# First-stage attention scores in float32 from 64-row halves, and transposes as pairs of 64-row halves

## The chip, the cores and the metric

One core of a Trainium2 chip runs the whole program. The metric is device microseconds (us) of one execution; smaller is better. The engines are called as the profile calls them: PE is TensorE (matmuls), PEld its weight loads, DVE VectorE, ACT ScalarE, POOL GpSimd, SP SyncE (here it only issues DMAs).

## The reference

Two attention stages follow each other. The first has 8 batches of 8 heads, 576 positions, head width 64, and keeps only scores within `tau` of the row's maximum. Its output, 512 wide per position, goes into a mixture of four causal attention experts, of which each position takes the best two.

```
scores = scale * q @ k.T                      # stage 1, per batch and head
thresh = max(scores) - tau
scores = where(scores >= thresh, scores, -1e9)
attn = exp(scores - max); attn /= sum(attn) + 1e-9
x = (attn @ v), heads side by side            # (8, 576, 512)

logits = x @ w_gate; top 2 of 4 experts, weights w by softmax
for e in range(4):                            # stage 2, per batch
    q, k, v = x @ wq[e], x @ wk[e], x @ wv[e]
    a = softmax(scale * q @ k.T, causal)
    out += (e in top 2) * w * (a @ v @ wo[e])
```

## The kernel before

**Tiles.** Stage 1 works on 32 pairs of heads, four per batch. The 576 positions are four tiles of 128 queries (s = 0 to 3) and a tail of 64, and the tails of the two heads make one tile of 128 rows (s = 4). For each pair `prep` (L827) loads q and k, `scores` (L903) makes scores, maximum, threshold, exponential and normalised weights, `transp` (L945) and `transp_tails` (L958) transpose the weights on PE and copy them out of PSUM with ACT, and `attnv` (L972) multiplies them with v. After the four pairs of a batch, `moe` (L1222) runs stage 2 for that batch: projections, values and gate, then for two pairs of experts (ep) and five query tiles `scores2` (L1110), `transp2` (L1151) and `attnv2`, and `output`.

**Scores before.** From the third pair on (`DIRECT = 2`) q and k are transposed on PE, split into a rounded high part and a rest (`hl`, ACT and DVE in `split`), and spread by DMA (`spread_keys`, `spread_queries`) into `qt` and `kt`, so that one matmul with 128 rows multiplies both parts of q with one part of k. A tile s < 4 takes, for each head, four such matmuls of 288 columns in the one-pass format fp32r; s = 4 takes six. Each head of a tile has its own two PSUM banks (family `s`) and its own place in the order. The first two pairs (`first`, L777) go another way: plain float32, head 0 in rows 0 to 63 and head 1 in rows 64 to 127 of the array, four matmuls of 64 rows for a tile; the chip gets a float32 matmul as two instructions, so that the trace shows eight.

**Stage 2 scores before.** `spread2` (L1052) spreads the parts of q and k by DMA in the same manner; a head of a tile takes two fp32r matmuls with 128 rows.

**Transposes before.** A 128x128 block is one `transpose` (L594): the block is the stationary operand, the identity moves through it, 128 columns. Four blocks fill one PSUM bank (family `g`), which one ACT copy empties.

**Order.** The functions only record operations. `Plan.arrange` then gives each engine's instructions an order and each tile a buffer, from a modelled cost of each operation and from places (`PLACE`, `PLACE_OP`), numbers that say how early each unit of work ranks. All matmuls into one PSUM tile form a group that PE runs in one piece; PE may take groups up to three places out of order (`AHEAD`). A group starts when its PSUM banks are free: there are eight of 2 KB per partition. In the profile all matmuls have line L591 and all transposes L1282; DMAs have L688 and L690.

Of the kernel before, what the change touches and what calls it, by code (L numbers as in the profile page):

```python
# [22 lines left out]
SLOTS = {"ki": 1, "qi": 1, "tm": 2, "hl": 1, "qt": 2, "kt": 2, "pp": 4, "st": 2, "vm": 2, "p2": 3, "pt": 10,  # L23
         "ptt": 2, "x": 12, "v2": 1, "q2": 2, "q2x": 1, "k2x": 1, "zt": 2, "z0": 2, "z1": 2, "pt2t": 1}
PLACE = {
# [45 lines left out]
}  # L71
PLACE_OP = {
    "ACT gw": -1.321, "ACT hl": -2.1489, "ACT lg": 0.5171, "ACT p2": -0.0353, "ACT pp": 0.2646, "ACT pt": 0.2207,
    "ACT ptt": -0.0387, "ACT q2": 1.5521, "ACT q2d0": 4.5817, "ACT q2d1": 1.7694, "ACT tau_t": -0.2988,
    "ACT tm": -1.4854, "ACT v2": 1.2109, "ACT warm": -1.1366, "ACT wkh": 0.8714, "ACT woh": 1.1122,
    "ACT wqh": 1.1708, "ACT wvh": 1.067, "ACT x": -0.5607, "ACT z0": 1.1015, "ACT z1": -0.3179, "ACT zt": 0.2316,
    "DVE col": 0.6337, "DVE g": -1.4561, "DVE gate": -1.9949, "DVE gt": -3.3295, "DVE gw": 0.1335,
    "DVE hl": -3.6827, "DVE lg": 2.0741, "DVE p2": 0.0604, "DVE pp": -1.0396, "DVE pt": -0.5423,
    "DVE pt2t": 1.7323, "DVE q2": 0.9391, "DVE qsc": -0.1751, "DVE s": -0.5422, "DVE st": -1.8452,
    "DVE still": -0.1359, "DVE tau_n": -1.4713, "DVE v2": -0.8112, "DVE warm": -2.9831, "DVE x": 0.2785,  # L80
    "DVE z0": -0.7041, "DVE z1": -2.1009, "DVE zt": 0.323, "POOL col": 0.0444, "POOL hl": 1.0723,
    "POOL ident": -1.4208, "POOL mask": -3.3156, "POOL mask2": -1.1591, "POOL p2": 0.2278, "POOL pp": 1.6676,
    "POOL pt2t": 0.6725, "POOL q2d0": 1.5757, "POOL q2d1": 1.1287, "POOL qd0": 1.6629, "POOL qd1": 1.472,
    "POOL qi": 2.1477, "POOL st": 0.0218, "POOL tie": -1.6109, "POOL tm": -0.3646, "POOL vtz0": 0.7892,
    "POOL vtz1": -0.4386, "POOL wkl": 1.9586, "POOL wol": 0.1773, "POOL wql": 3.2786, "POOL wvh": 1.4077,
# [62 lines left out]
class Op:  # L148
    def __init__(self, e, busy, late, outs, ins, fn, at):
# [1163 lines left out]
```

## Time and profile before

| | us |
|---|---|
| runs of the kernel, median of 3 (lowest, highest) | 914.93 (914.17, 915.96) |
| span of the profiled execution, first to last instruction | 911.6 |
| PE, PEld busy | 892.5, 832.6 |
| DVE, ACT, POOL busy | 734.2, 651.4, 442.7 |

The profile gives its execution by the span. The median of the runs is 3.3 us above it, which is what lies around the span. Busy time of PE counts a matmul from its start to its modelled end, and matmuls overlap; what one costs in a stream is the distance from its start to the start of the next.

### The profile page before, as it was taken

How to read it: one execution, taken by the hardware profiler on the slowest of the kernel's cores; microseconds unless marked ns; L12 is line 12 of the kernel's file. 1: busy time of each engine (PE TensorE's matmuls, PEld its weight loads, DVE VectorE, ACT ScalarE, POOL GpSimd, SP SyncE). 2: the span in 40 equal slices, each digit the busy share in tenths (PEclk: the TensorE clock that was granted, in tenths of full speed). 3: DMA queues.
4: the chain of work that ended last, by engine and by line, in shares of the span. 5: the costliest groups of instructions: out<-in, count | busy, mean ns of one | idle time of the engine just before them, and what ended most of it. 6: DMA issues, size and time to landing. Idle time of an engine off the chain costs nothing.

```text
span 911.6 us, 26016 instructions
## 1 busy us (share of the span) xinstructions
PE 892.5 (98%) x9218; PEld 832.6 (91%) x9218; DVE 734.2 (81%) x2139; ACT 651.4 (71%) x1542; POOL 442.7 (49%) x905
## 2 busy tenths in 40 slices
PE   7899999999999999999999999999999999999998
PEld 5589999899999999999999999999999999999986
DVE  6887778896888869888698877988778886888375
ACT  4787668775778757887587865888667875777454
POOL 5867436553455535555255543555435653445101
PEclk9999999999999999999999999999999999999999
DMA  7625474554565554754546555564474554561151
GB/s 175 163 68 139 116 173 102 142 140 110 143 157 136 135 127 104 189 147 116 127 104 175 127 127 144 127 168 121 103 181 116 141 143 117 138 153 42 36 140 59
DMA packets 147650, 117.86 MB, mean 129 GB/s; under 512 B 99008, under 2 KB 107456, under 8 KB 147520
## 3 DMA queue, kind: packets, MB, share of 16 engines
q1 hardware_dynamic: 146176, 115.90, 51.6%
q8 instruction: 73, 1.20, 0.6%
q10 hardware_dynamic: 1344, 0.30, 0.2%
q14 instruction: 57, 0.47, 0.2%
HBM read 30.42 MB, written 9.44 MB: 44 GB/s over the span
## 4 chain that ended last, share of the span: by engine, by line
PE 81%; DVE 6%; ACT 4%; SPq 3%; DMA 2%; issue 2%; POOL 1%; DVEq 0%; ACTq 0%
PE banks L591 60%; PE banks L1282 20%; SPq L688 2%; ACT pp L678 2%; DMA k2x<-q 1%; DVE pp L662 1%; ACT p L678 1%; DVE col L648 1%; ACT pt L612 1%; DVE gt L614 1%; SPq L690 0%; DVE banks L667 0%; DVE gw L623 0%; DVE q L623 0%; DVE x L623 0%
## 5 line engine op out<-in xcount | busy, mean ns | idle before, releaser
L640 POOL TENSOR_SCALAR pp<-pp,col 128x576 f32<-128x576 f32 x278 | 205.5, 749 | 171.3 <-DVE col L651 132.6
L648 DVE TENSOR_REDUCE col<-banks 128x1 f32<-128x576 f32 x304 | 227.1, 751 | 34.5 <-PE banks L591 31.9
L662 DVE SCALAR_TENSOR_TENSOR pp<-banks,col,pp 128x576 f32<-128x576 f32 x278 | 223.6, 813 | 29.9 <-ACT pp L678 17.1
L612 ACT ACTIVATE pt<-banks 128x512 f32<-128x512 f32 (+2 forms) x400 | 223.1, 590 | 32.9 <-PE banks L1282 29.4
L678 ACT ACTIVATE pp<-banks,col 128x576 f32<-128x576 f32 x284 | 207.2, 740 | 40.0 <-DVE col L648 36.1
L1282 PE MATMUL banks<-ident,pp 128*128 128x128 f32 x1281 | 186.4, 274 | 3.0 <-DVE p L662 1.8
L591 PE MATMUL banks<-kt,qt 128*128 128x288 f32 x960 | 174.9, 311 | 0.4 <-DMA tm<-in_k_dram 0.3
L640 POOL TENSOR_SCALAR col<-col,tau_n 128x1 f32<-128x1 f32 x288 | 77.0, 268 | 193.9 <-DVE col L648 150.3
L1282 PEld LDWEIGHTS banks<-ident,pp 128*128 128x128 f32 x1281 | 148.7, 140 | 13.6 <-issue 3.8
L591 PE MATMUL banks<-pt,vm 128*64 128x128 f32 (+1 forms) x2560 | 154.6, 264 | 0.0
L591 PEld LDWEIGHTS banks<-kt,qt 128*128 128x128 f32 x960 | 136.0, 189 | 6.1 <-issue 3.1
L591 PEld LDWEIGHTS banks<-pt,vm 128*64 128x64 f32 x2560 | 131.3, 137 | 7.7 <-issue 4.3
L678 ACT ACTIVATE p<-banks,col 128x256 f32<-128x256 f32 (+4 forms) x142 | 78.7, 561 | 33.1 <-DVE col L667 18.5
L640 POOL TENSOR_SCALAR p<-p,col,gw 128x384 f32<-128x384 f32 (+3 forms) x117 | 71.6, 621 | 57.1 <-ACT p L678 32.5
L612 ACT ACTIVATE x<-banks 128x256 fp32r<-128x256 f32 (+1 forms) x96 | 28.3, 329 | 70.5 <-PE banks L591 70.5
L1282 PE MATMUL banks<-ident,p 128*128 128x128 f32 x404 | 63.2, 276 | 3.3 <-POOL p L640 1.8
L591 PE MATMUL banks<-wvh,x 128*128 128x260 f32 x320 | 64.2, 284 | 0.0
L667 DVE CUSTOM_DVE_ANT_0 banks<-banks,mask 128x384 f32<-128x384 f32 (+3 forms) x128 | 61.9, 500 | 2.4 <-PE banks L591 1.3
L591 PE MATMUL banks<-ptt,vtz 128*64 128x128 f32 (+1 forms) x640 | 58.9, 262 | 0.0
L623 DVE TENSOR_TENSOR x<-banks,x 128x256 fp32r<-128x256 f32 (+1 forms) x96 | 31.9, 353 | 31.2 <-ACT x L612 30.8
L639 DVE TENSOR_SCALAR col<-col 128x2 f32<-128x2 f32 (+1 forms) x240 | 47.8, 202 | 10.4 <-ACT p L678 8.0
L1282 PEld LDWEIGHTS banks<-ident,p 128*128 128x128 f32 x404 | 47.1, 141 | 9.3 <-POOL p L640 3.0
(139 smaller groups left out, 1558.2 us busy)
## 6 DMA issues: line engine op xcount, KB each, us to landing
kt<-hl SPq DMA_DIRECT2D x240, 144.0 KB, 2.6
k2x<-q SPq DMA_DIRECT2D x128, 128.0 KB, 2.4
qt<-hl SPq DMA_DIRECT2D x120, 128.0 KB, 2.4
vm<-in_v_dram SPq DMA_DIRECT2D x32, 256.0 KB, 3.1
q2x<-q SPq DMA_DIRECT2D x64, 128.0 KB, 2.4
qi<-in_q_dram SPq DMA_DIRECT2D x60, 128.0 KB, 2.5
ki<-in_k_dram SPq DMA_DIRECT2D x60, 128.0 KB, 3.0
out_dram<-st SPq DMA_DIRECT2D x30, 256.0 KB, 2.5
```

The lines of the kernel that those rows point to most:

```text
L591: lambda o, x, y: nc.tensor.matmul(o, x, y, start=start, stop=stop))
L612: run(e, t, [dst], [src], lambda d, s: nc.scalar.activation(d, s, AF.Copy))
L614: run(e, t, [dst], [src], lambda d, s: nc.vector.tensor_copy(d, s))
L623: lambda d, a, b: (nc.vector if e == "DVE" else nc.gpsimd).tensor_tensor(d, a, b, op=op))
L639: return m.tensor_scalar(d, s, x_, None, op0=op0)
L640: return m.tensor_scalar(d, s, x_, y_, op0=op0, op1=op1)
L648: lambda d, s: nc.vector.tensor_reduce(d, s, axis=axis, op=op, **({"negate": True} if negate else {})))
L662: return nc.vector.scalar_tensor_tensor(d, a_, x_, r.pop(0), op0=op0, op1=op1, **kw)
L667: lambda o, a, i, m: nc.vector.tensor_tensor_reduce(o, i, m, 1.0, 3e38, ALU.add, ALU.min, a))
L678: return nc.scalar.activation(d, s, AF.Exp, scale=scale, **kw)
L688: fn = lambda d, s: q_.dma_start(d.bitcast(F32), s.bitcast(F32))
L1282: o.fn(*(r.place() for r in (*o.outs, *o.ins)))
```

## The change

The special path for the first two pairs goes, and every pair takes one path: q and k (and their tails, loaded into the diagonal blocks of the 128x128 tiles `tk` and `tq`, which hold zeros elsewhere) are transposed, copied by ACT into `kx` and `qx` (ACT multiplies q by the scale on the way), and multiplied in float32 from 64-row halves, both heads of a tile side by side, in one group of four PSUM banks. The tail tile uses 64-column halves of the array instead. A transpose of a 128x128 block becomes two of 64 rows each, into two banks, which two ACT copies empty into interleaved columns. The second stage multiplies its fp32r parts in place, three products for each head from 64-row halves, with no spreading. The transposes of s = 4 go together with the tails of the first group, and those of the second stage are grouped by `T2_GROUPS`. The places are other numbers throughout; `SLOTS` has other buffers (five `pp` instead of four).

```diff
+    def transposed(x, y, blocks):
+        for n, (a, b) in enumerate(blocks):
+            for o, i, sl in ((x, a, heads[0]), (y, b, heads[1])):
+                half_transpose(o[:, n * D:(n + 1) * D], i[sl], sl)
+    def half_transpose(o, x, rows):
+        plan.op("PE", 30, 30 + 217 + 35, [o], [x, ident[rows, rows]], nc.tensor.transpose)
...
     def prep(n):
-        hl = plan.tile("hl", [P, 2, 2 * SM + 3 * ST], F32R)
...
+        for j in range(2):
+            dma(tk[heads[j], heads[j]], k[b, 2 * hp + j, SM:, :], "SP", more)
...
+            if x is ki:
+                transposed(*gs, list(zip([*cs, tail], [tail, *cs])))
+            else:
+                transposed(*gs, [(c, c) for c in (*cs, tail)])
...
+                copy("ACT", d, g, None if x is ki else qsc)
     def scores(n, s, qk):
+        sp = [plan.tile("s", [P, 2, 512], F32) for _ in range(nj)]
+        sp[-1].v.first = sp[0].v
+        for hf in range(2):
+            for j, rows in enumerate(heads):
+                o = hf * HS + (ST if j == 0 else 0)
+                if s < R:
+                    matmul(sp[j][:, hf, :HS], qx[rows, s * P:(s + 1) * P], kx[rows, o:o + HS], True, True)
+                else:
+                    matmul(sp[0][rows, hf, :HS], qx[:, SM + j * ST:SM + (j + 1) * ST], kx[:, o:o + HS], True, True)
...
+    def blocks_out(blocks, out):
+        gs = [gbank() for _ in range(2)]
+        gs[1].v.first = gs[0].v
+        transposed(*gs, blocks)
+        w = len(blocks) * D
+        for i, g in enumerate(gs):
+            copy("ACT", out[:, :2 * w].rearrange("p (n c) -> p n c", c=P)[:, :, i * D:(i + 1) * D],
+                 g[:, :w].rearrange("p (n c) -> p n c", c=D))
     def transp(n, s, pp):
+        cols = [j * (S + ST) + c * P for j in range(2) for c in range(R)]
+        return blocks_out([(pp[:, o:o + P],) * 2 for o in cols], plan.tile("pt", [P, 2 * SM], F32))
...
-    def spread2(qs, ks):
...
     def scores2(b, t, ep, q2, gates, place):
+            for i, (x, y) in enumerate(HHL):
+                for g, rows in zip(gs, heads):
+                    matmul(g, q2[0][rows, x, t * P:w], q2[1][rows, y, :w], i == 0, i == 2)
...
+T2_GROUPS = ((4,), (3,), (2,), (1, 0))
```

## Rows read from the trace of the kernel before

**Rows 1.** The page: span, and busy time of each engine.

```profile
span 911.6 us, 26016 instructions
PE 892.5 (98%) x9218; PEld 832.6 (91%) x9218; DVE 734.2 (81%) x2139; ACT 651.4 (71%) x1542; POOL 442.7 (49%) x905
```

**Rows 2.** Windows: stretch, length, busy PE, PEld, DVE, ACT, POOL, clock, DMA, GB/s.

```profile
279.80:389.00 109.20, 109.06 (x1150) 103.78 (x1150) 90.76 (x265) 80.13 (x191) 53.88 (x110) 1.00 0.55 136
825.80:911.60 85.80, 79.70 (x766) 72.05 (x762) 50.94 (x171) 47.92 (x132) 18.20 (x31) 1.00 0.24 66
...
20.00:40.00 20.00, 15.67 (x90) 10.04 (x86) 17.41 (x48) 14.19 (x29) 15.14 (x32) 1.00 0.68 169
```

**Rows 3.** Groups by form: transposes on PE, the two largest and the smallest.

```profile
L1282 PE MATMUL banks<-ident,pp 128*128 128x128 f32 x1281 | 186.4, 274 | 3.0 <-DVE p L662 1.8 <-ACT ptt L612 0.6 <-POOL pp L640 0.3
...
L1282 PE MATMUL banks<-ident,p 128*128 128x128 f32 x404 | 63.2, 276 | 3.3 <-POOL p L640 1.8 <-ACT pt L612 0.6 <-POOL col L640 0.4
...
L1282 PE MATMUL banks<-ident,pt 128*128 128x128 f32 x16 | 2.5, 278 | 2.3 <-DVE pp L662 1.6 <-DMA pt<-in_k_dram 0.7
```

**Rows 4.** Groups by form: weight loads (PEld) of transposes, scores and weights times v.

```profile
L1282 PEld LDWEIGHTS banks<-ident,pp 128*128 128x128 f32 x1281 | 148.7, 140 | 13.6 <-issue 3.8 <-DVE p L662 2.0 <-POOL pp L640 1.7
L591 PEld LDWEIGHTS banks<-kt,qt 128*128 128x128 f32 x960 | 136.0, 189 | 6.1 <-issue 3.1 <-ACT x L612 0.6 <-DVE pp L662 0.6
L591 PEld LDWEIGHTS banks<-pt,vm 128*64 128x64 f32 x2560 | 131.3, 137 | 7.7 <-issue 4.3 <-DVE pp L662 1.1 <-ACT pt L612 0.5
```

**Rows 5.** Timeline of PE: transposes, scores of a tile, scores of a tail.

```profile
281.77 1.04 PE L1282 MATMUL banks<-ident,p 128*128 128x128 f32 x8
282.64 0.60 PE L1282 MATMUL banks<-ident,pp 128*128 128x128 f32 x4
...
302.69 1.03 PE L591 MATMUL banks<-hl,qd 128*128 128x288 f32 x6
303.56 0.40 PE L591 MATMUL banks<-woh,zt 128*128 128x512 f32 x1
...
339.67 0.60 PE L1282 MATMUL banks<-ident,pp 128*128 128x128 f32 x4
340.03 1.30 PE L591 MATMUL banks<-kt,qt 128*128 128x288 f32 x8
341.17 1.04 PE L1282 MATMUL banks<-ident,pp 128*128 128x128 f32 x8
```

**Rows 6.** Timeline of PE: from transposes into 64-column matmuls.

```profile
505.17 0.60 PE L1282 MATMUL banks<-ident,pp 128*128 128x128 f32 x4
505.70 0.69 PE L591 MATMUL banks<-pt,v 128*64 128x64 f32 x16
506.22 0.29 PE L591 MATMUL banks<-pt2t,v 128*64 128x64 f32 x4
506.33 1.05 PE L591 MATMUL banks<-pt,v 128*64 128x128 f32 x16
507.21 1.04 PE L591 MATMUL banks<-pt,vm 128*64 128x128 f32 x16
```

**Rows 7.** Timeline of PE: a float32 score tile of the second pair, 64-row halves.

```profile
40.33 1.24 PE L591 MATMUL banks<-p,pt 64*128 64x288 f32 x8 [0.22 <-DVE pp L662]
41.50 1.09 PE L591 MATMUL banks<-pt,vm 128*64 128x128 f32 x16
```

**Rows 8.** Timeline of PE: second-stage scores of 256 columns.

```profile
355.23 0.64 PE L591 MATMUL banks<-k2x,q2x 128*128 128x256 f32 x4
355.71 0.60 PE L1282 MATMUL banks<-ident,pp 128*128 128x128 f32 x4
```

**Rows 9.** Groups by form: work of DVE and ACT on q and k, and ACT's copy of transposes.

```profile
L623 DVE TENSOR_TENSOR hl<-banks,hl 128x512 fp32r<-128x512 f32 x60 | 40.8, 686 | 2.1 <-ACT hl L612 2.1
...
L612 ACT ACTIVATE hl<-banks 128x512 fp32r<-128x512 f32 x60 | 35.8, 605 | 4.2 <-PE banks L1282 3.5
...
L612 ACT ACTIVATE pt<-banks 128x512 f32<-128x512 f32 x352 | 203.7, 607 | 30.0 <-PE banks L1282 26.6 <-DVE col L639 1.4 <-ACT pt L612 0.5
```

More of the change, by code (lines that the diff above doesn't have):

```diff
@@ L71 @@
 }
 PLACE_OP = {
[L73 to L82, printed above, removed]
@@ new lines @@
+    "ACT q2d1": -0.1661, "ACT qi": -3.6815, "ACT qx": 1.0489, "ACT tau_t": 0.1675, "ACT tq0": 1.6009, "ACT v2": 3.767,
+    "ACT warm": 3.146, "ACT wkh": 2.5436, "ACT woh": -2.5484, "ACT wqh": -0.4803, "ACT wvh": 3.6375, "ACT x": -0.5738,
+    "ACT z0": 1.9112, "ACT z1": -0.3273, "ACT zt": 4.0564, "DVE col": 0.6684, "DVE g": -0.0805, "DVE gate": -2.3704,
+    "DVE gt": -0.2416, "DVE gw": 1.9262, "DVE lg": 0.1698, "DVE p2": 1.1878, "DVE pp": 0.0112, "DVE q2": 3.7093,
+    "DVE qsc": -2.675, "DVE s": 1.8996, "DVE st": -1.5353, "DVE still": -1.4634, "DVE tau_n": 3.7129,
@@ L89 @@
+    "POOL wkl": -1.3291, "POOL wol": 1.8582, "POOL wql": -0.6015, "POOL wvh": -3.1776, "POOL wvl": -2.4348,
+    "SP ki": 0.5207, "SP lg": 0.763, "SP out": -2.1432, "SP qi": 0.7356, "SP st": -0.842, "SP tk0": 1.6704,
+    "SP tk1": -3.9139, "SP tq0": 1.8877, "SP tq1": -0.4887, "SP vm": -0.9968, "SP vtx0": -0.7429, "SP vtx1": -1.1194,
+    "SP vtz0": -1.0997, "SP vtz1": 0.0673,
 }
@@ L297, in network @@
             needs[g] = [v for v in dict.fromkeys(needs[g]) if ops[g].e == "PE" or v not in early]
-        return members, of, busy, shift, done, narrow, net, after, users, needs, ends
+        return members, of, busy, shift, done, mode, net, after, users, needs, ends
     def writers(self, v):
@@ L304, in arrange @@
         ops, tiles = self.ops, self.virtuals
-        members, of, busy, shift, done, narrow, net, after, users, needs, ends = self.network()
+        members, of, busy, shift, done, mode, net, after, users, needs, ends = self.network()
         rank = {g: (ops[g].key + (PLACE_OP.get(ops[g].kind, 0.0) if ops[g].e != "PE" else 0.0), g) for g in members}
@@ L607, with copy @@
     inps = lambda *xs: any(x.v.fams[0] in ("s", "g") for x in xs)
-    def copy(e, dst, src):
+    def copy(e, dst, src, scale=None):
         t = cost(e, size(src), inps(src))
-        if e == "ACT":
+        if scale is not None:
+            run(e, t + 90, [dst], [src, scale], lambda d, s, x: nc.scalar.activation(d, s, AF.Copy, scale=x))
+        elif e == "ACT":
             run(e, t, [dst], [src], lambda d, s: nc.scalar.activation(d, s, AF.Copy))
@@ L685, in dma @@
         a, b = isinstance(dst, Ref), isinstance(src, Ref)
-        late = (4100 if a and dst.v.fams[0] in ("kt", "qt") else 3800) + more
+        late = (4100 if a and dst.v.fams[0] in ("-",) else 3800) + more
         if a and b:
@@ L724 @@
     wol = const("wol", [P, EP, DM], F32R)
-    qds = [const(f"qd{i}", [P, 2, P], F32R) for i in range(2)]
     vtz = [const(f"vtz{i}", [P, 2, D]) for i in range(2)]
+    vtx = [const(f"vtx{i}", [P, 2, D]) for i in range(2)]
+    tks = [const(f"tk{i}", [P, P]) for i in range(2)]
+    tqs = [const(f"tq{i}", [P, P]) for i in range(2)]
     q2ds = [const(f"q2d{i}", [P, 2, P], F32R) for i in range(2)]
-    for t in qds:
-        memset("POOL", t.bitcast(F32), 0.0)
-    for t in vtz:
+    for t in (*tks, *tqs, *vtz, *vtx):
         memset("POOL", t, 0.0)
@@ L822, in values_in @@
         dma(vm, v[b, 2 * hp:2 * hp + 2, :SM, :].rearrange("h (p r) d -> p h r d", r=R))
-        for j, rows in enumerate(heads):
-            dma(vtz[n % 2][rows, j], v[b, 2 * hp + j, SM:, :])
-        return vm, vtz[n % 2]
+        for j in range(2):
+            dma(vtz[n % 2][heads[j], j], v[b, 2 * hp + j, SM:, :])
+            dma(vtx[n % 2][heads[1 - j], j], v[b, 2 * hp + j, SM:, :])
+        return vm, vtz[n % 2], vtx[n % 2]
     def prep(n):
         b, hp = divmod(n, NPAIR)
-        if n < DIRECT:
-            return first(n)
@@ L853, in prep @@
-        ki, qi = ms
-        plan.place = (n, "perm")
-        ql = tl[:ST].rearrange("p j d -> p (j d)")
-        scaled("POOL", ql, ql, qsc[:ST], 0.0, ALU.mult, ALU.add)
-        hl = plan.tile("hl", [P, 2, 2 * SM + 3 * ST], F32R)
-        qt = plan.tile("qt", [P, 2, SM], F32R)
-        kt = plan.tile("kt", [P, 2, 2, S], F32R)
-        qd = qds[n % 2]
-        def split(cols, g):
-            copy("ACT", hl[:, 0, cols], g)
-            minus("DVE", hl[:, 1, cols], g, hl[:, 0, cols].bitcast(F32))
@@ L866, in main @@
-        def main(m, o):
-            g = gbank()
-            for r in range(R):
-                transpose(g[:, r * P:(r + 1) * P], m[:, r].rearrange("p j d -> p (j d)"))
-            split(slice(o, o + SM), g)
-        def spread_keys(j):
-            o = KO if j else KO + ST
-            for x in range(2):
-                for rows in heads:
-                    dma(kt[rows, j, x], hl[heads[j], x, o:o + S])
-        def spread_queries(j):
-            for x, rows in enumerate(heads):
-                dma(qt[rows, j], hl[heads[j], x, :SM])
@@ L882, in prep @@
-        plan.place = (n, "kT")
-        main(ki, KO + ST)
-        plan.place = (n, "tT")
-        g = gbank()
-        transpose(g[:, :P], tl.rearrange("p j d -> p (j d)"))
-        split(slice(SM, SM + 2 * ST), g[:, :P])
-        copy("POOL", hl[:, :, KO + S:], hl[:, :, KO:KO + ST].bitcast(F32))
-        for j, sl in enumerate(heads):
-            copy("POOL", qd[sl, :, j * ST:(j + 1) * ST], hl[sl, :, SM:KO].bitcast(F32))
-        spread_keys(0)
-        plan.place = (n, "qT")
-        main(qi, 0)
@@ L894, in prep @@
-        spread_queries(0)
-        spread_keys(1)
-        spread_queries(1)
-        return (qt, kt, qd, hl[:, :, KO + ST:], *values_in(n))
+        ki, qi = (plan.tile(name, [P, R, 2, D], F32) for name in ("ki", "qi"))
+        tk, tq = tks[n % 2], tqs[n % 2]
+        ks = k[b, hs, :SM, :].rearrange("h (p r) d -> p r h d", r=R)
+        qs = q[b, hs, :SM, :].rearrange("h (r p) d -> p r h d", r=R)
+        eq = "SP" if n else "ACT"
+        more = 0 if n > 1 else 100
+        plan.place = (n if n else -30.0, "load")
@@ new lines, in prep @@
+        for j in range(2):
+            dma(ki[:, :, j], ks[:, :, j], "SP", more)
+        plan.place = (n if n else -29.0, "qload" if n else "load")
+        for j in range(2):
+            dma(qi[:, :, j], qs[:, :, j], eq, more)
+        plan.place = (n if n else -22.0, "tload" if n else "load")
+        for j in range(2):
+            dma(tk[heads[j], heads[j]], k[b, 2 * hp + j, SM:, :], "SP", more)
+        for j in range(2):
+            dma(tq[heads[j], heads[j]], q[b, 2 * hp + j, SM:, :], eq, more)
@@ L943, in scores @@
         return pp
-    def transp(n, s, pp):
-        pts = []
-        for j in range(2 if s < R else 1):
-            plan.place = (n, f"t{s}{j}")
-            g = gbank()
-            o = j * J1
-            for c in range(R):
-                transpose(g[:, c * P:(c + 1) * P], pp[:, o + c * P:o + (c + 1) * P])
-            pt = plan.tile("pt", [P, SM], F32)
-            copy("ACT", pt, g)
-            pts.append(pt)
-        return pts
-    def transp_tails(tiles, pp):
+    def blocks_out(blocks, out):
+        gs = [gbank() for _ in range(2)]
+        gs[1].v.first = gs[0].v
+        transposed(*gs, blocks)
[3 more added lines that the diff above has]
+                 g[:, :w].rearrange("p (n c) -> p n c", c=D))
+        return out
@@ new lines, in transp @@
+    def transp(n, s, pp):
+        plan.place = (n, f"t{s}0")
+        cols = [j * (S + ST) + c * P for j in range(2) for c in range(R)]
+        return blocks_out([(pp[:, o:o + P],) * 2 for o in cols], plan.tile("pt", [P, 2 * SM], F32))
+    def transp_tails(tiles, pp):
+        main = [s for s in tiles if s < R]
+        blocks = [(pp[s][:, SM:SM + P],) * 2 for s in main]
+        if R in tiles:
+            p = pp[R]
+            blocks = [(p[:, c * P:(c + 1) * P], p[:, ST + c * P:ST + (c + 1) * P]) for c in range(R)] + blocks
+            blocks.append((p[:, S - P:S], p[:, :P]))
+        return blocks_out(blocks, plan.tile("pt4" if R in tiles else "ptt", [P, len(blocks) * P], F32))
@@ L959, in transp_tails, with attnv @@
+    def attnv(tiles, qk, pt, ptt, xs):
+        vm, vt, vx = qk[2:]
         g = gbank()
         main = [s for s in tiles if s < R]
-        w = len(main) * P
-        ptt = plan.tile("ptt", [P, 3 * P], F32)
+        first = R * P if R in tiles else 0
         for s in tiles:
-            o = main.index(s) * P if s < R else w
-            transpose(g[:, o:o + P], pp[s][:, SM:SM + P] if s < R else pp[s][:, S - P:S])
-        copy("ACT", ptt[:, :w], g[:, :w])
-        if w < len(tiles) * P:
-            for i in range(2):
-                copy("ACT", ptt[i * ST:(i + 1) * ST, w:w + ST], g[ST:, w + i * ST:w + (i + 1) * ST])
@@ L1050, in projected @@
         return res
-    def spread2(qs, ks):
-        q2x, k2x = plan.tile("q2x", [P, 2, SM], F32R), plan.tile("k2x", [P, 2, 2, SM], F32R)
-        for j, sl in enumerate(heads):
-            for x, rows in enumerate(heads):
-                for dst, src in ((q2x[rows, j], qs[sl, x, :SM]), (k2x[heads[0], j, x], ks[sl, x, :SM]),
-                                 (k2x[heads[1], j, x], ks[sl, x, :SM])):
-                    dma(dst, src)
-        return q2x, k2x
     def values(b, base, pre, parts):
```

237 lines of the change are left out of this document (77 added, 160 removed), and 72 rows, old and new, of tables (PLACE, PLACE_OP).

## Prediction

> **What bounds the kernel now.** I read the page first: PE is busy 98% of the span, DVE 81%, ACT 71%, POOL 49% [rows 1]. Then the windows: cut at one period of a batch, 109.2 us, they show PE busy for 109.06 of it at clock 1.00, while DVE has 90.76, ACT 80.13 and POOL 53.88 [rows 2]. So in the steady part the time of a batch is what PE has to do for it, and DVE has 18 us of room. Only the ends differ: between 20 and 40 us PE is busy 15.67 of 20, in the last 85.8 us 79.70 [rows 2]. Last the timeline of PE, where the distance between starts says what each kind of work takes. An edit is therefore priced by what it takes from or gives to PE. DMAs, POOL and the split of q and k count only if they made PE late, and in the period shown PE had 0.14 us without work.
>
> **The sum.** The page gives the span, 911.6; I add the changes to the median, 914.9, which holds the 3.3 us around it.
>
> *Transposes.* Eight take 282.64 - 281.77 = 0.87 us, 0.109 each [rows 5]. There are 50 for each of 32 pairs and 50 for each of 8 batches, 2000 in all (seven groups, of which the two largest and the smallest are shown [rows 3]): 218.0 us. After the change a pair has 5 + 5 blocks of q and k, 32 of weights and 7 + 2 for the tails, 51, and a batch's stage 2 still 50: 2032 blocks, each two half transposes. No row has a half transpose. It moves 64 columns instead of 128, so alone it should take 0.109 / 2 = 0.0545; if the two halves of the array work side by side, a block takes that once. Upper bound: 0.109 for a block, no overlap. Lower bound: the nearest rows of small paired work, 64-column matmuls with a weight load each, four in 506.33 - 506.22 = 0.11 us, 0.028 each [rows 6], 0.055 for a block. That 64-row halves do overlap is in the trace too: eight float32 instructions of 288 columns in one group take 41.50 - 40.33 = 1.17 us [rows 7], 0.98 without the change of array form priced below, 0.122 each, where two passes of 288 columns at the transpose's rate of 0.109 for 128 would take 0.245 alone. So I take a value near the lower end, 0.030 for a half, 0.060 for a block: 2032 x 0.060 = 121.9, **-96.1 us**.
>
> The weight loads could spoil this, since a half transpose still loads 128 columns. A load of 128 columns takes 189 ns for the scores, one of 64 columns 137 [rows 4], so 64 columns more cost 52 ns; but a transpose's load of 128 columns takes 140 [rows 4], hardly more than the one of 64. I read that as some 55 ns of loading, which hides behind the 54.5 ns of moving.
>
> The Trainium skill, page "TensorE: Matmul & The Clock Gate", section "LDWEIGHTS (loading the stationary operand)", says that a load takes its columns divided by 1.2, in ns, whatever the number of rows. By it a half would load for 107 ns, two side by side would make a block 107 ns, and the sum below would end at an estimated 946 us. The scores' loads agree with the rule (52 ns for 64 columns), the transposes' loads at 140 ns do not.
>
> *First-stage scores.* Eight fp32r matmuls take 341.17 - 340.03 = 1.14 us, of which 0.08 are still the transposes ahead of them (their last start is not followed by the usual 0.109: four stand in 0.36 us instead of 0.44): 1.06 for the two heads of a tile [rows 5]. The new tile takes 0.98, as above. 30 pairs of four tiles change (the first two pairs do it already): 120 x -0.08 = **-9.6**. The tail took six matmuls in 0.87 - 0.08 = 0.79 us [rows 5]; now eight instructions on 64-column halves: sixteen of 128 columns take 507.21 - 506.33 = 0.88, 0.055 each [rows 6], so 288 columns 0.124 and eight 0.99: 30 x 0.20 = **+6.0**.
>
> *Second-stage scores.* Four matmuls of 256 columns take 0.48 us, 0.12 each [rows 8]. By width, 512, 384 and 128 columns get 0.24, 0.18 and 0.11 (near a full weight load): four of each, 2.6 us for a pair of experts. Three products from half the array, two heads side by side, stand against two from the whole: three quarters of that. 16 x -0.65 = **-10.4**.
>
> *Changes of array form.* This is the price of the change, and the trace shows it only between other forms. From transposes to 64-column matmuls: 505.70 - 505.17 is 0.53, four transposes are 0.44, so 0.09 pass; then sixteen matmuls take 0.52 instead of 16 x 0.028 = 0.45, 0.07 more [rows 6]. So 0.16 for a change. Between 64-row halves and the rest the row shows 1.17 for about 0.98 of work, 0.19 for what lies inside one visit [rows 7]. I take 0.16, with 0.09 and 0.20 as ends. The count: before, a batch goes into the 64-column form and back nine times, 18 changes, in the period from 279.80. Laying the new forms over the same order of groups (transposes and the scores of s < 4 and t < 4 in 64-row form, tails and weights times v in 64-column form, projections, values, stage 2's tail scores and output whole) I count 54. 36 x 8 x 0.16 = **+46.1** (26 to 58).
>
> *What costs nothing.* The spreading DMAs go, and a few small loads for `tk`, `tq` and `vtx` come for each pair; POOL loses the scaling and the block-diagonal copies; DVE loses 2 x 686 ns for a pair [rows 9], 5.5 us a batch, 85.3 left of 90.8. ACT copies eight blocks of weights in two copies of 512 columns as before, 607 ns each [rows 9], and the tails in four copies as before; q and k take four copies of 320 columns (607 ns each at most) where they had two of 605 [rows 9]: at most 1.2 us more for a pair, 5 for a batch, 85 of some 101. All of this lies beside PE's work. If PE's lead were gone, DVE and ACT would be next at 85 us a batch.
>
> *Ends.* At the start and in the last stage PE is not full, so part of the gain is lost there: those 147 us would gain 8.0 x 147 / 109.2 = 10.8, of which I count half as lost, **+5**.
>
> Sum: -96.1 - 9.6 + 6.0 - 10.4 + 46.1 + 5 = -59.0. 914.9 - 59.0 = **856 us**, about 102 us for a batch. With the ends of halves (0.055 to 0.07 for a block: -10 to +20) and changes of form (-20 to +12), the forecast's own range is 836 to 876.
>
> **Rivals.** *The half transposes are no faster for a block than a whole one* (slower than before). If their loads go at the scores' rate, 104 ns for 128 columns, or the halves run one after the other, a block takes 0.104 to 0.109, transposes give 7 us less to 3 us more, and the other terms add 32: 940 to 950, I take **942**. It decides from 0.0915 a block, 46 ns a half, on: there the sum is zero. For it: no row has a half transpose, and it still loads 128 columns. Against it: the 140 ns of rows 4 and the overlap of rows 7.
>
> *PSUM becomes the wait.* Both heads of a tile are one group and need four of the eight banks at once, and a transpose group two instead of one. The four come free only when DVE has read them for the last time; if PE can then never make the next tile ahead, DVE idles for the 1.2 us of a tile [rows 7], 20 tiles a batch: 85.3 + 24 = 109.3, no gain. DVE has other work for part of that; half way between 101 and 109.3, 105.3 a batch, gives 914.9 - 8 x 3.9 = **884**. The skill's page "TensorEngine Tiling (Array Packing)", section "Gotcha 1: PSUM Pressure", names the same cost of row tiling. For it: DVE is at 83% of the period. Against it: a score tile holds its banks some 4 us, and one is due every 5.
>
> *Fewer changes of form.* If the new order keeps equal forms together, 30 instead of 54: 24 x 8 x 0.16 = 31 less, **825**.
>
> **How the numbers follow.** Chances: forecast 0.68, PSUM 0.15, slower 0.11, fewer changes 0.06. The range 822 to 895 takes the forecast, the fewer changes and most of PSUM, and leaves out the slow case and PSUM's upper part. A measurement of this kernel tells about 0.2%, 1.8 us, from no change. Faster 0.88, same 0.01 (PSUM at its upper end), slower 0.11.
>
> **What would show it.** Right: blocks of half transposes at 55 to 65 ns by their starts, PE still over 95% busy, a batch of about 102 us, some 50 changes of form in it at 0.15 us. Half transposes 46 ns or more apart make it wrong at the first step; PE waiting for DVE's reads of score banks (DVE's multiply ahead of score groups among PE's waits) would be the second rival. A DVE busy share above PE's, or ACT's copies ending late ahead of weights times v, would show another bound than I priced.

## The result and the profile after

The changed kernel takes 923.12 us (median of 10 runs, 919.3 to 928.05), the kernel before 914.8 beside it (10 runs, 913.16 to 916.04): a ratio of 1.0094, interval 1.0069 to 1.012. The change made it slower by 0.9%, where 856 us was forecast, and 923 lies outside the range.

The page of the changed kernel (span; busy time of each engine; PE's granted clock in 40 slices), to be read beside [rows 1]:

```profile
span 925.8 us, 29385 instructions
PE 865.9 (94%) x11489; PEld 726.8 (79%) x11489; DVE 672.6 (73%) x2021; ACT 655.7 (71%) x1560; POOL 385.3 (42%) x757
...
PEclk9888999899999999999999999989999999999999
```

PE was busy 98% and is now at 94%, and no other engine took its place: DVE and POOL lost busy time, as forecast. (The profiled execution took 927.6 us, 4.5 above the median.) Two things are new. PE has no matmul in flight for 925.8 - 865.9 = 59.9 us (before 19.1), and its clock is no longer full: the mean granted clock is 0.959, so (1 - 0.959) x 925.8 = 38.0 us of full-speed work are lost. Among the ten executions that is the upper end: their clocks go from 0.959 to 0.971, and the one with a span of 918.4 us at 0.971 lost 26.6. A window shows it in the middle of the run too (stretch, length, busy PE, PEld, DVE, ACT, POOL, clock, DMA, GB/s), where before had clock 1.00 and PE busy for all but 0.14 us of a batch [rows 2]:

```profile
170.00:280.00 110.00, 104.75 (x1428) 89.02 (x1428) 82.95 (x251) 81.17 (x193) 46.17 (x90) 0.97 0.17 45
```

What PE waits for stands in its waits (us in total, times, longest); the transposes are now L1168, matmuls L575, DVE's multiply by the threshold mask L659, ACT's copies L609:

```profile
PEld banks L1168 <- DVE pp L659: 44.2, 45, 2.4
...
PE banks L1168 <- DVE pp L659: 32.0, 29, 1.9
...
PEld banks L575 <- ACT pt L609: 30.3, 62, 1.5
...
PE banks L575 <- ACT pt L609: 9.4, 15, 1.4
```

The like of the second line in the kernel before, where it is the largest of PE's waits:

```profile
PE banks L1282 <- DVE pp L662: 1.9, 2, 1.6
```

(PE's waits and its loads' are in part the same time, so the lines don't add up.) Transposes that wait for DVE's multiply don't need its result here: they wait for PSUM banks that it still reads. One such place in the timeline (start, us, what, with the idle time ahead of it and what ended it):

```profile
523.58 2.21 PE L575 MATMUL banks<-kx,qx 64*128 64x288 f32 x16
...
524.85 2.09 DVE L645 TENSOR_REDUCE col<-banks 128x1 f32<-128x576 f32 x3 [0.47 <-PE banks L575]
525.70 2.04 ACT L675 ACTIVATE pp<-banks,col 128x576 f32<-128x576 f32 x3 [2.13 <-DVE col L645]
...
526.85 0.81 DVE L659 SCALAR_TENSOR_TENSOR pp<-banks,col,pp 128x576 f32<-128x576 f32 x1
...
527.72 0.27 PE L1168 MATMUL banks<-ident,ki 64*128 64x64 f32 x1 [1.94 <-DVE pp L659]
...
528.77 0.72 PE L1168 MATMUL banks<-ident,qi 64*128 64x64 f32 x3 [0.53 <-ACT kx L609]
```

Sixteen score instructions are two tiles, four banks each: all eight. The next transposes, those of the following pair's k (`ki`), need two banks, and the first come free when DVE has found the maxima, ACT has taken the exponential and DVE has multiplied. PE stands for 1.94 us, works for about half a microsecond, and stands for 0.53 again, for ACT's copy of k. The windows around it show what follows:

```profile
523.20:528.60 5.40, 3.12 (x28) 1.86 (x27) 4.44 (x8) 2.72 (x5) 2.06 (x6) 1.00 0.35 97
528.60:535.40 6.80, 6.62 (x56) 4.34 (x56) 3.17 (x11) 4.67 (x10) 3.14 (x6) 0.50 0.40 88
535.40:540.00 4.60, 4.60 (x85) 4.05 (x84) 4.07 (x11) 2.58 (x7) 0.66 (x3) 1.00 0.04 8
```

After 5.4 us of which PE was busy 3.12, the clock is at 0.50 for 6.8 us (1.2 instead of 2.4 GHz), though PE is full again. The timeline of PE shows it too. A tail's scores in that stretch take twice what they take at full clock (sixteen instructions in 535.62 - 531.45 = 4.17 us, against eight in 560.94 - 559.92 = 1.02):

```profile
531.45 4.25 PE L575 MATMUL banks<-kx,qx 128*64 128x288 f32 x16
535.62 0.69 PE L575 MATMUL banks<-pt,vm 128*64 128x64 f32 x16
...
559.92 1.19 PE L575 MATMUL banks<-kx,qx 128*64 128x288 f32 x8
560.94 0.64 PE L575 MATMUL banks<-pt,vm 128*64 128x64 f32 x16
```

So these waits cost their own length and, behind them, half of 6.8, some 3.4 us of work.

The work itself came out as priced. Where PE is fed, half transposes start 31 to 34 ns apart (eight in 556.40 - 556.15 = 0.25 us, thirty in 557.49 - 556.47 = 1.02 with the change of form behind them), 0.030 forecast. The timeline of PE:

```profile
555.57 0.29 PE L575 MATMUL banks<-x,wql 128*128 128x288 f32 x1
555.79 0.27 PE L1168 MATMUL banks<-ident,ki 64*128 64x64 f32 x1
...
556.15 0.41 PE L1168 MATMUL banks<-ident,qi 64*128 64x64 f32 x8
556.40 0.22 PE L1168 MATMUL banks<-ident,tq 64*128 64x64 f32 x2
556.47 1.09 PE L1168 MATMUL banks<-ident,pp 64*128 64x64 f32 x30
557.49 1.06 PE L575 MATMUL banks<-q,q2d 128*128 128x288 f32 x6
```

By the rule on loads that the prediction cites from the Trainium skill (page "TensorE: Matmul & The Clock Gate", section "LDWEIGHTS (loading the stationary operand)") a half would take 107 ns to load and a block as much. These rows show 62 to 68 ns for a block, so for transposes the measurement decides against the rule.

### The profile page after: what moved, and what is told of

It reads as the page before. It is cut to its first block, busy times and chain, and to the rows that moved or that the text cites. A ratio compares the mean times of both kernels' runs of the same rounds, so it can differ in the third digit from the quotient of the medians.

```text
span 925.8 us, 29385 instructions
## 1 busy us (share of the span) xinstructions
PE 865.9 (94%) x11489; PEld 726.8 (79%) x11489; DVE 672.6 (73%) x2021; ACT 655.7 (71%) x1560; POOL 385.3 (42%) x757
## 4 chain that ended last, share of the span: by engine, by line
PE 81%; DVE 9%; ACT 5%; issue 3%; POOL 2%; DMA 0%; SPq 0%; DVEq 0%; ACTq 0%; POOLq 0%
PE banks L575 66%; PE banks L1168 15%; DVE pp L659 4%; ACT pp L675 3%; DVE col L645 3%; ACT pt L609 1%; POOL pp L637 1%; PE banks L1165 1%; ACT p L675 1%; DVE st L611 0%; DMA lg<-in_moe_w_gate_dram 0%; POOL p L637 0%; POOL col L637 0%; DVE p L637 0%; ACT kx L609 0%
## 5 line engine op out<-in xcount | busy, mean ns | idle before, releaser
L675 ACT ACTIVATE pp<-banks,col 128x576 f32<-128x576 f32 (+2 forms) x291 | 208.8, 740 | 92.7 <-DVE col L645 90.5
L659 DVE SCALAR_TENSOR_TENSOR pp<-banks,col,pp 128x576 f32<-128x576 f32 x284 | 226.1, 814 | 39.9 <-ACT pp L675 31.8
L609 ACT ACTIVATE pt<-banks 128x512 f32<-128x512 f32 (+3 forms) x448 | 224.8, 569 | 38.5 <-PE banks L1168 34.4
L575 PE MATMUL banks<-kx,qx 64*128 64x288 f32 (+1 forms) x1280 | 213.3, 445 | 9.9 <-ACT pt L609 7.7
L575 PEld LDWEIGHTS banks<-kx,qx 64*128 64x128 f32 (+1 forms) x1280 | 120.5, 187 | 54.5 <-ACT pt L609 19.3
L575 PE MATMUL banks<-pt,vm 128*64 128x128 f32 (+1 forms) x2560 | 154.3, 264 | 0.0
L575 PEld LDWEIGHTS banks<-pt,vm 128*64 128x64 f32 x2560 | 132.8, 138 | 15.1 <-issue 6.2
L1168 PE MATMUL banks<-ident,pp 64*128 64x64 f32 x2626 | 122.8, 237 | 6.0 <-POOL col L637 1.7
L1168 PEld LDWEIGHTS banks<-ident,pp 64*128 64x128 f32 x2626 | 103.2, 148 | 25.1 <-issue 9.7
L664 DVE CUSTOM_DVE_ANT_0 banks<-banks,mask 128x128 f32<-128x128 f32 (+3 forms) x128 | 61.0, 511 | 17.4 <-PE banks L575 16.4
L575 PE MATMUL banks<-wvh,x 128*128 128x260 f32 x320 | 63.4, 288 | 0.0
L609 ACT ACTIVATE x<-banks 128x256 fp32r<-128x256 f32 (+1 forms) x96 | 28.2, 329 | 39.5 <-PE banks L575 38.0
L575 PEld LDWEIGHTS banks<-wvh,x 128*128 128x128 f32 x320 | 51.1, 188 | 5.9 <-issue 5.6
L575 PE MATMUL banks<-x,wqh 128*128 128x288 f32 x256 | 53.3, 300 | 0.0
L575 PE MATMUL banks<-x,wkh 128*128 128x288 f32 x256 | 53.1, 300 | 0.0
L575 PE MATMUL banks<-pt,v 128*64 128x128 f32 (+1 forms) x960 | 50.5, 258 | 1.6 <-ACT pt L609 1.6
```

Source lines behind the costliest of these rows:

```text
L575: lambda o, x, y: nc.tensor.matmul(o, x, y, start=start, stop=stop))
L609: run(e, t, [dst], [src], lambda d, s: nc.scalar.activation(d, s, AF.Copy))
L659: return nc.vector.scalar_tensor_tensor(d, a_, x_, r.pop(0), op0=op0, op1=op1, **kw)
L664: lambda o, a, i, m: nc.vector.tensor_tensor_reduce(o, i, m, 1.0, 3e38, ALU.add, ALU.min, a))
L675: return nc.scalar.activation(d, s, AF.Exp, scale=scale, **kw)
L1168: o.fn(*(r.place() for r in (*o.outs, *o.ins)))
```

## The experiments

The theory: PE's work costs what the sum says; the rest is waits for PSUM banks that the softmax of a score pair holds, and the half clock after them. To test it, the span of each run is taken apart in one way: off it go PE's idle time (span less busy) above the 19.1 us of before, and (1 - clock) x span. What is left is counted as work. Two limits of this sum: PE's idle time at half clock goes off twice (3.3 us in the changed kernel), and the control e6, which has PE's work of before, is left with 905.8 instead of 911.6, so a difference of some 6 us says nothing.

| run | median us | span | PE idle | lost to clock | left |
|---|---|---|---|---|---|
| before | 914.8 | 911.6 | 19.1 | 0 | 911.6 |
| changed kernel | 923.1 | 925.8 | 59.9 | 38.0 | 847.0 |
| e1_threshold_from_sbuf | 907.9 | 906.8 | 55.8 | 20.9 | 849.2 |
| e4_fill_idle | 919.1 | 918.7 | 59.6 | 28.5 | 849.7 |
| e5_multiply_cut | 897.5 | 895.5 | 51.0 | 13.4 | 850.2 |
| e10_max_and_multiply_cut | 883.4 | 882.1 | 44.8 | 7.9 | 848.5 |
| e11_softmax_cut | 870.0 | 867.8 | 35.5 | 5.2 | 846.2 |
| e3_whole_transposes | 990.8 | 989.6 | 57.4 | 35.6 | 915.7 |
| e7_exp_before_max | 931.5 | 930.7 | 58.8 | 11.2 | 879.8 |
| e8_exp_before_max_new_order | 917.8 | 917.3 | 51.3 | 8.3 | 876.8 |
| e9_new_order_alone | 996.3 | 1000.8 | 97.7 | 53.0 | 869.2 |
| e12_no_threshold_op_new_order | 897.8 | 895.6 | 38.4 | 4.5 | 871.8 |
| e2_threshold_from_sbuf_before | 926.5 | 925.8 | 27.7 | 5.6 | 911.6 |
| e6_multiply_cut_before | 910.8 | 908.8 | 18.5 | 3.6 | 905.8 |

### Cutting the softmax, one pass at a time

Four runs keep PE's instructions and their order and take one thing after the other from what holds the banks. In the first, DVE's multiply compares the exponentials in SBUF with exp(-tau) (`tau_e`) instead of the scores in PSUM with the threshold, which gives the banks back one pass earlier; POOL still makes the threshold:

```diff
+    def kept(e, sv, th, sm):
+        run("DVE", cost("DVE", size(e), True, True), [e, sm], [sv, th, e, tau_e],
+            lambda d, acc, a, x, y, t: nc.vector.scalar_tensor_tensor(d, y, t, y, op0=ALU.is_ge, op1=ALU.mult, accum_out=acc))
...
-            stt(e, sv, thr[:, js], e, ALU.is_ge, ALU.mult, accum=ss[:, js])
+            kept(e, sv, thr[:, js], ss[:, js])
```

The plan still books the operation as a reader of the scores (`sv`), so the order stays as it was.

> Kernel after, same order, same buffers, same PE work; DVE's multiply compares the exponentials (in SBUF) with exp(-tau) instead of the scores (in PSUM) with max - tau, so a score bank is free when ACT's exponential has ended, about 0.9 us earlier. Theory PSUM (PE is starved because it waits for banks that DVE still reads; the half clock follows from these gaps): PE's waits for DVE's multiply (44 us before weight loads, 32 before matmuls) go, time falls by 15 to 45 us, to 878 to 908. Rival clock (half transposes by themselves do not hold the clock): half clock stays at 75 us, time 915 to 925. Rival changes of form (334 of them at 0.19 us are the loss): time 915 to 925.

907.91 us, ratio 0.9923 (0.9895 to 0.995): faster than both kernels, and at the upper end of what the theory gave. This is the run that tells the banks from the chain of results: the banks come back a pass earlier, while the chain from scores to weights gets no shorter. Among PE's waits those for DVE's multiply are gone, and ACT's copies come last instead:

```profile
PEld banks L575 <- ACT pt L609: 39.3, 81, 1.5
...
PE banks L1174 <- ACT kx L609: 17.1, 16, 1.6
...
PE banks L575 <- ACT pt L609: 13.1, 27, 1.4
```

Then the multiply on 2 of 576 columns, which leaves out the masking and the sums of the rest (against the run before):

```diff
-            lambda d, acc, a, x, y, t: nc.vector.scalar_tensor_tensor(d, y, t, y, op0=ALU.is_ge, op1=ALU.mult, accum_out=acc))
+            lambda d, acc, a, x, y, t: nc.vector.scalar_tensor_tensor(d[:, :, :1], y[:, :, :1], t, y[:, :, :1], op0=ALU.is_ge, op1=ALU.mult, accum_out=acc))
```

> Kernel after, same order and buffers, but DVE's multiply by the threshold is done on 2 of the 576 columns only, from SBUF (the rest of the masking and of the sums is left out): 288 passes of 0.81 us become short, no score bank waits for DVE's second pass, and nothing new uses POOL's port. PE's work is that of after. Theory PSUM/DVE wait (PE starved by banks that DVE reads late): most of the 55 us without work on PE and of the 37 us lost to the half clock goes, 850 to 885. If PE's own work with its changes of form holds the time: 905 or more.

897.51 us, ratio 0.9817 (0.9797 to 0.9838): the way of the theory, but less than the 850 to 885 it gave. Then the maximum too, over 2 columns:

```diff
+    def least(dst, src):
...
+            lambda d, s: nc.vector.tensor_reduce(d, s[:, :, :1], axis=AX.XY, op=ALU.max, negate=True))
...
-            reduce(nmx[:, js], sv, AX.XY, ALU.max, negate=True)
+            least(nmx[:, js], sv)
```

> The changed kernel, same order and buffers, with both of DVE's passes over the first-stage scores cut: the maximum is taken over 2 of a row's 576 columns, and the multiply by the mask covers 2 columns (masking, row sums and the true maximum are left out; ACT still takes the exponential of all columns). A pair of score banks now waits for ACT's exponential alone. Theory (the banks of a score pair are held through DVE's passes): with the multiply cut 897.5, now PE's waits at the transposes of q and k and at score tiles shrink again, to a time of 865 to 885. Rival (it is ACT: its copies of q, k and of transposed weights come late because ACT itself is full or ordered so, and DVE has nothing to do with it): 890 to 900, as with the multiply cut alone.

883.38 us, ratio 0.9651 (0.9635 to 0.9667), at the upper end of what the theory gave and below what the rival gave. Then the exponential on 2 columns, with POOL writing the weights from a constant:

```diff
+    def few(dst, src, bias):
...
+            lambda d, s, b: nc.scalar.activation(d[:, :, :1], s[:, :, :1], AF.Exp, bias=b, scale=1.0))
...
+    def flat(p, x):
...
+            lambda d, s, x, o: nc.gpsimd.tensor_scalar(d, o, x, 0.0, op0=ALU.mult, op1=ALU.add))
...
-            exp(e, sv, bias=nmx[:, js])
+            few(e, sv, nmx[:, js])
...
-            scaled("POOL", p, p, ss[:, h:h + 1], 0.0, ALU.mult, ALU.add)
+            flat(p, ss[:, h:h + 1])
```

> As the run before, and ACT's exponential covers 2 of 576 columns as well, and POOL writes the weights from a constant (the first stage's softmax is left out but for its instructions, their order, and POOL's full-width write). PE's own instructions and their order are those of the changed kernel; ACT has 190 us less to do. Theory (the sum of PE's work in the forecast is right, and what it lacked are waits and the half clock that follows them): PE is fed, the clock stays at full, and the time is what the sum of PE's work and of its changes of form make, 815 to 850. Rival (the half transposes, score tiles or changes of form cost more than the sum has, wherever they stand): 865 or more, with PE busy and at full clock.

869.99 us, ratio 0.9511 (0.9495 to 0.9527). By its number alone this is the rival's case, above 865, and outside the 815 to 850 of the theory. The profile says otherwise: PE is busy 832.3 of 867.8 us, so still idle for 35.5 (before 19.1), and its two largest waits are for ACT's copies, which these cuts leave in. The page, and these waits:

```profile
PE 832.3 (96%) x11489; PEld 707.8 (82%) x11489; DVE 360.7 (42%) x2021; ACT 515.5 (59%) x1561; POOL 386.2 (45%) x758
```

```profile
PE banks L575 <- ACT pt L609: 9.3, 15, 1.4
PE banks L1188 <- ACT kx L609: 8.3, 9, 2.9
```

The steps are 25.6 us for the multiply (923.1 to 897.5), 14.1 for the maximum, 13.4 for the exponential: 53 of the 67 that were missing to 856. In all of them, and in the changed kernel, 846 to 850 us of work are left. Only idle time and clock went. For the maximum and the exponential the time that the banks are held and the chain to the weights got shorter together, so these two steps don't tell one from the other.

The multiply cut in the kernel before is the control:

> The same cut in the kernel before, as a control: DVE loses 230 us of work. PE is the bound there, so 905 to 917; if DVE's second pass held this kernel too, below 895.

910.83 us, ratio 0.9962 (0.9948 to 0.9977). The pass that costs the changed kernel 25.6 us costs the one before 4: there PE was the bound, and DVE's passes lay beside it.

### PE's work by itself

Whole transposes for the 1408 blocks of weights that come in even groups (1088 of the first stage, 320 of the second), in the same order and the same banks:

```diff
+    def whole_transpose(o, x):
+        plan.op("PE", 60, 60 + 217 + 35, [o], [x, ident], nc.tensor.transpose)
...
+        if len(blocks) % 2 == 0:
...
+            for n, (a, _) in enumerate(blocks):
+                whole_transpose(gs[n // k][:, n % k * P:(n % k + 1) * P], a)
```

> Kernel after with 1408 of its 2032 blocks transposed whole (128 rows, 128 columns), in the same places of the order and into the same banks; PE's own work grows by 1408 x 0.049 = 69 us, and up to 100 more changes of form at 0.16 add 16. If PE's work sets the end: 995 to 1010. Theory PSUM: part of it falls into the 55 us in which PE has nothing in flight and into half-clock time that goes: 945 to 975. Rival clock: half clock falls below 30 us, gives back 25 or more: 965 to 985.

990.8 us, ratio 1.0834 (1.0806 to 1.0862): 67.7 us more than the changed kernel. Put in were 1408 x (0.109 - 0.060) = 69.0 of PE work by the forecast's price, 58 to 66 by the 62 to 68 ns measured for a block, and 117 more changes of form (451 against 334, counted in PE's timeline), some 19 to 23 at 0.16 to 0.2 each: 77 to 89 together. PE's idle time and the clock's loss hardly move (59.9 to 57.4, 38.0 to 35.6). So the half transposes do bring about what was forecast, and most of the work that PE is spared comes off the end, though PE isn't full. The theory had expected more of it to fall into the idle time (945 to 975) and missed; presumably the waits stand at fixed places in the order and take little of it in, which no run here tests.

The other way to keep the clock up is to give PE matmuls of no use while it waits; the kernel has such fillers at its start.

```diff
-    idle = plan.fill(1250.0, 80000.0, 9000.0, 110.0, 217.0)
+    idle = plan.fill(1250.0, 1000000.0, 9000.0, 110.0, 217.0)
```

> Kernel after with idle PE time of over 0.7 us in the written order filled with small bf16 matmuls into free banks up to the end (before: up to 80 us only). Rival clock: the clock stays at its upper level, 75 us of half clock go, 25 to 37 us gained, 886 to 898. Theory PSUM: the clock is only part: half clock falls by half, 5 to 18 us gained, 905 to 918, and the gaps in which PE waits for DVE stay.

919.11 us, ratio 1.0052 (1.0034 to 1.0071). Only 11 more fillers found a place (11500 matmuls against 11489): a filler needs a PSUM bank as well, and where PE waits for banks there is none (behind 80 us the kernel's own plan has 30 idle stretches of PE that are long enough, and a bank is free in one of them). The time, outside both expectations, is that of the changed kernel's shorter executions (919.3 to 920.4 us, clock 0.968 to 0.971; here 0.969 to 0.973): inconclusive on what a full clock alone would give.

### Freeing the banks at less cost

The threshold from SBUF in the kernel before:

> The same edit in the kernel before, as a control. Theory PSUM: PE is never without work there, so nothing comes of it, 912 to 917. If the edit helps by itself (DVE's operand, not the bank), it gains here as much as in e1.

926.54 us, ratio 1.0131 (1.0108 to 1.0154): slower, where the theory gave 912 to 917. By the table all of it is idle PE and clock, and PE's waits for POOL went from 3.0 us in all to 11.4. POOL's column operation before, in this run, in the changed kernel and in e1 (groups by line; mean ns of one behind the busy time):

```profile
L640 POOL TENSOR_SCALAR col<-col,tau_n 128x1 f32<-128x1 f32 x288 | 77.0, 268 | 193.9 <-DVE col L648 150.3 <-DVE col L639 21.6 <-DVE col L651 17.3
```

```profile
L640 POOL TENSOR_SCALAR col<-col,tau_n 128x1 f32<-128x1 f32 x288 | 129.3, 450 | 166.4 <-DVE col L648 129.7 <-DVE col L639 16.2 <-DVE col L651 13.3
```

```profile
L637 POOL TENSOR_SCALAR col<-col,tau_n 128x1 f32<-128x1 f32 x288 | 75.7, 265 | 180.2 <-DVE col L645 170.3 <-DVE col L648 5.5 <-DVE col L636 3.1
```

```profile
L637 POOL TENSOR_SCALAR col<-col,tau_n 128x1 f32<-128x1 f32 x288 | 115.5, 403 | 148.9 <-DVE col L645 140.5 <-DVE col L648 4.3 <-DVE col L636 2.8
```

When DVE's multiply reads two operands from SBUF instead of one from PSUM and one from SBUF, POOL's 128x1 operation goes from 268 to 450 ns in the kernel before and from 265 to 403 in the changed one, and the multiply itself from 813 to 879 and from 814 to 839. With the multiply on 2 columns (e5) POOL's mean is 266.

Giving the banks back after ACT's pass alone, by taking the exponential before the maximum:

```diff
-            reduce(nmx[:, js], sv, AX.XY, ALU.max, negate=True)
...
-            exp(e, sv, bias=nmx[:, js])
...
+            exp(e, sv)
+            reduce(nmx[:, js], e, AX.XY, ALU.max)
...
```

> The changed kernel with the first stage's softmax turned round: ACT takes the exponential straight from the scores in PSUM, without the row's maximum; DVE then finds the maximum, and multiplies by the threshold mask, on the exponentials in SBUF; POOL makes the threshold as maximum times exp(-tau). Same sums, same order of places, same buffers. A pair of score tiles now holds its PSUM banks for one ACT pass (about 0.45 us a tile) instead of a DVE pass, a POOL op and an ACT pass. Theory (a pair's four banks are held through the softmax, and PE waits for them at fixed places): the waits of PE for DVE's and ACT's first-stage passes shrink, PE idle and half clock fall below those of the run with the threshold from SBUF (50.7 and 41 us), and the time lies at 885 to 905, that is under its 907.9. Rival one (what holds PE is the order of the copies on ACT, not the banks): as that run, 905 to 912. Rival two (both of DVE's passes now read SBUF and slow POOL's column ops, whose mean went from 265 to 403 ns when one of them did): 912 or more.

931.49 us, ratio 1.0177 (1.0162 to 1.0191). As the second rival had it. PE's waits for DVE's multiply are gone, those for ACT's exponential are short, and the clock is at 0.988. But the transposes now wait for POOL's normalising: the chain from scores to normalised weights got longer. The first two of PE's waits, and POOL's groups:

```profile
PE banks L1170 <- POOL pp L637: 12.3, 17, 2.4
PE banks L575 <- ACT pp L675: 5.3, 14, 0.9
```

```profile
L637 POOL TENSOR_SCALAR pp<-pp,col 128x576 f32<-128x576 f32 x284 | 222.6, 792 | 163.0 <-DVE col L648 107.2 <-PE banks L1170 21.1 <-DVE gate L645 17.4
L637 POOL TENSOR_SCALAR col<-col,tau_e 128x1 f32<-128x1 f32 x288 | 118.4, 412 | 231.0 <-DVE col L645 167.1 <-DVE col L636 36.3 <-DVE col L648 26.5
```

The same with other places, so that work lies closer where banks are free early, and those places in the changed kernel:

```diff
...
-    "av1": 1.5198, "kT": -1.1766, "later": -2.409, "load": -2.2168, "perm": 3.2453, "qT": -1.1682, "qload": -2.1062,
...
+    "av1": 1.5082, "kT": -1.171, "later": -1.5431, "load": -2.6448, "perm": 3.2453, "qT": -1.16, "qload": -1.9084,
...
```

> The same as the kernel with the exponential before the maximum, with another order of the work: the numbers that place each step of a batch among those of the others are set anew for banks that come free early (steps of the first-stage scores lie closer together, loads earlier); nothing else differs. Theory (PSUM's hold time and the order that was fitted to it together keep PE from being fed): PE idle falls under 30 us and half clock under 25 us, time 870 to 890, faster than the kernel before (914.8) and than every run so far (897.5 with DVE's multiply cut). Rival (changes of the array form and PE's own work are the bound, and the order can't give back anything): within 1% of the kernel with the old order.

> The changed kernel's own arithmetic (maximum first, read from PSUM) with the new order of the run with the exponential before the maximum. If the order by itself were the gain, this would be as fast as that run, 870 to 890. If the order only serves once the banks come free early, as the theory has it, PE waits longer than in the changed kernel: 930 to 1000, with PE idle over 60 us.

917.79 us, ratio 1.0032 (1.0017 to 1.0047), and 996.27, ratio 1.0904 (1.0875 to 1.0933). The second came out as expected: in the changed kernel those places cost 73 us, with 97.7 us of idle PE and clock 0.947. The order that is the better one with banks free early is much the worse with banks held long. The first missed both of its expectations: 14 us better than the old order, still no gain. In the table it is left with 877 us, some 30 more than the changed kernel. At most 8 of them are changes of form (41 more, at 0.2), and 6.5 are 59 more fillers, of 0.11 us each. Some 5 more are short waits: the profile counts a transpose as busy for 0.22 to 0.27 us, so a shorter wait behind one doesn't show as idle, and at full clock two transposes of one form start more than 0.15 us apart 77 times here, 49 times in the changed kernel (117 times in e7, 12 us more of it, beside 100 more fillers). The other 10 us were not settled. As e9 is left with 869, most of the 30 come with the order.

Last, the threshold from SBUF without POOL's operation, which that comparison doesn't need, and with places of its own:

```diff
-            scaled("POOL", thr[:, js], nmx[:, js], -1.0, tau_n, ALU.mult, ALU.add)
...
-            stt(e, sv, thr[:, js], e, ALU.is_ge, ALU.mult, accum=ss[:, js])
+            stt(e, e, tau_e, e, ALU.is_ge, ALU.mult, accum=ss[:, js])
...
```

> A version meant to beat both. DVE's multiply compares the exponentials in SBUF with exp(-tau), as in the run with the threshold from SBUF, but POOL's threshold op, whose mean rose to 403 ns there, is gone altogether, and the places of the steps are set anew for it. Theory (banks come free one DVE pass earlier, and POOL's slow column op left the chain): under the 907.9 of that run, 885 to 905. Rival (DVE's reads of SBUF and POOL's normalising slow each other and the chain to the transposed weights gets longer, as in the runs with the exponential before the maximum, 931 and 918): 908 or more.

897.77 us, ratio 0.9812 (0.9797 to 0.9826): 1.9% faster than before, and by the medians 2.7% faster than the change. The window that had clock 0.97 and 104.75 us of busy PE in the changed kernel, and POOL's largest group:

```profile
170.00:280.00 110.00, 106.89 (x1484) 90.38 (x1482) 88.15 (x256) 82.80 (x199) 44.35 (x56) 1.00 0.18 48
```

```profile
L637 POOL TENSOR_SCALAR pp<-pp,col 128x576 f32<-128x576 f32 x284 | 245.2, 874 | 386.0 <-DVE col L648 330.3 <-PE banks L575 24.5 <-PE banks L1169 20.3
```

What the operation and the new places each bring of the 10 us against e1 was not tried apart. POOL's normalising takes 874 ns where the changed kernel has 743 and e1, with the same reads of DVE, 748; why it is the normalising that is slow in this order was not tried either.

## Why the prediction was wrong

- **The sum of PE's work was right.** It said -64 us of work (-59 with the +5 for the ends); the table has 911.6 - 847.0 = 64.6, good to some 6 us. That it comes so close is in part luck, as single terms were off and cancel: the timeline has 334 changes of form against 169 before, 42 a batch instead of 54, so some +26 to +33 for the 165 new ones at an estimated 0.16 to 0.2 us each, instead of +46.1; the transposes are 31 to 34 ns a half instead of 30, which takes 4 to 16 us back.
- **The step that failed is "What costs nothing".** It set DVE, ACT and POOL to zero because "all of this lies beside PE's work", judging by busy time: DVE at 85 of 102 us a batch. What decided was not how busy DVE is but how long its passes, with ACT's between them, hold the score banks: cutting the first stage's softmax pass by pass gave 53 us back. The idle PE of 40.8 us more and the 38.0 us lost to the clock, 78.8 together, turn a gain of 64.6 into a span 14.2 us longer.
- **The PSUM rival named the place, at too low a price.** It had four of eight banks a group, and 884 us, by DVE idling for 1.2 us a tile. Its argument against itself, that a tile holds its banks some 4 us and one is due every 5, is an average, and no row of the prediction shows the 4 us; the order puts two tiles in a row and the transposes of k behind them, and there all eight are held, 4.1 us from the first score matmul to the end of the multiply that frees the first two. The Trainium skill's page "TensorEngine Tiling (Array Packing)", section "Gotcha 1: PSUM Pressure", cited there, says that row tiling increases the pressure on PSUM. The trace agrees: 32.0 us of PE's waits and 44.2 of its loads' are for DVE's multiply. The prediction's own test was this line, DVE's multiply ahead of score groups; it stands ahead of transposes (32.0 us of PE's waits, against 1.5 ahead of all other matmuls).
- **The clock was not in the sum at all.** Before, it stood at 1.00 in every window read [rows 2], and the prediction carried that over to a kernel in which PE waits. In the profiled execution 38.0 of the 78.8 us stand there. With the order kept and the bank time cut step by step, it rises from 0.959 to 0.977, 0.985, 0.991 and 0.994. It seems to go with the long waits rather than with idle time in sum: e7 is idle for 58.8 us at 0.988, with 17 waits of 0.7 us as its largest kind where the changed kernel has 29 of 1.1.
- **The slow rival was wrong in its mechanism, though right that the kernel gets slower.** Half transposes are faster for a block by some 40%, and the kernel is slower all the same.
- **Chances.** 0.88 for faster rested on the share of PE's price that could be off, while the cover of the steps priced at zero had no term of its own.

## What to carry to other kernels

When a change makes the bound engine faster, price again everything that was hidden behind it, and for PSUM count bank time (banks times the whole chain from the first write to the last read), not the busy time of the readers. A wait of PE can be paid twice, once as idle time and once as a clock at half behind it, and busy time doesn't show the second part; the granted clock does. An order that was fitted to one holding time may have to be fitted again when the holding time changes.

## What was not expected of the hardware

- A stretch with PE busy for 3.12 of 5.4 us was followed by 6.8 us at clock 0.50, at full load; over the run the half clock took 38.0 us.
- DVE reading both operands of a 128x576 multiply from SBUF slows POOL: its 128x1 operation went from 268 to 450 ns and from 265 to 403, with a multiply of 2 columns back to 266. Its 128x576 one stayed at 748 in e1 (743 in the changed kernel) and took 874 in e12. DVE's own multiply went from 814 to 839 and 914 (e1 and e12), and from 813 to 879 (e2).
- Most of the work added to a PE that idles for 60 us came out in the time: an estimated 77 to 89 us put in, 67.7 measured.
